# The first two batches of an attention and channel-mixing kernel: from a scheduler's order to one written out by hand on four engines

## The chip, the core and the metric

The kernel runs on one core of a Trainium2 chip. The metric is device time in microseconds; before the change the median of three runs is 1208.21 us (1207.24 to 1208.43). The core's engines run side by side, each through its own list of instructions: TensorE (PE; its weight loads are PEld), VectorE (DVE), ScalarE (ACT), GpSimd (POOL) and SyncE (SP), which issues DMAs.

## The reference

```python
# q, k, v: 8 batches x 8 heads x 576 x 64; w_phi: 64 x 128
def phi(x):
    proj = x @ w_phi
    proj = proj - max(abs(proj), axis=-1)
    return concat([exp(proj), exp(-proj)])
q_p, k_p = phi(q), phi(k)
kv, z = k_p^T v, sum_s(k_p)                  # per head
attn = (q_p kv) / (q_p z + 1e-6)
x = attn as (batch, 576, 512)
u = x + ((x^T @ U) @ V)^T                    # U 576 x 32, V 32 x 576: tokens mix
out = u + max(u @ w_ch1, 0) @ w_ch2          # 512 -> 2048 -> 512: channels mix
```

The weights U, V, w_ch1 and w_ch2 come as float64 words, and the kernel turns them into 32-bit numbers itself.

## The kernel before

**Attention.** A "pair" is two heads of one batch: four pairs (j = 0 to 3) in each of eight batches. For a pair TensorE transposes the rows of k and q (tiles T; the last 64 rows of the sequence are a tile of their own, tail_T), multiplies by w_phi (pk, pkt for k; pq, pqt for q), and VectorE and ScalarE make the features: for k the maximum of the absolute values (L367), a subtraction (L369) and two exponentials; for q a copy out of the accumulator (L387, ScalarE), an all-reduce over partitions (L388, GpSimd), a subtraction (L389, VectorE) and two exponentials (L390, L391). Then come `s_kv` (kv_ps, copied by L487) and `s_out` (xp, divided into x by L510 to L522). From the third batch on (`split`) operands are made of a high and a low part, and T and tail_T of two halves each (L302, L303).

**Tokens.** When a batch's x is whole, `Tokens` splits it into xs (`split`, L584), multiplies by U (`down`: pp, pst) and by V (`up`: vp, added to x by L614). Each half of the channels has its own `split` and `down`.

**Mixer.** Its x is transposed into uT_hi and uT_lo (L234, L235). `hidden(f)` is 12 matmuls of 128x512 into the one accumulator bank `ph` (L642), then h_hi on ScalarE (L648) and h_lo on VectorE (L649); `add(f)` is 12 matmuls into four banks `o` (L661). There are 16 f in a batch, and one `hidden` or `add` is called a chunk below. The chunks of one batch are spread between the attention steps of the next one.

**Weight blocks.** The w_ch1 and w_ch2 of each f are two blocks, 32 in all, each loaded by one DMA of 512 KB. A block passes ScalarE (L141, L145), VectorE (L142, L147, L150: the words' parts into w_b and w_r), GpSimd (L155: the sum of w_b and w_r, a 64-bit integer add), ScalarE (L227: the high part w_hi) and VectorE (L228: the low part w_lo). They are converted once, while the first two batches run. U and V go the same way, but their sum is on VectorE (L157).

**Order.** The program is written as steps, and for the first two batches a scheduler sets the order of each engine's instructions, but for `narrow` (`s_out` and the next pair's `s_kv`), whose matmuls keep their place on PE. `mix` asks for the weight blocks of f+2 as it comes to chunk f, and `Pace` spreads 28 chunks over 20 steps of the next batch. From the third batch on (`ordered`), PE keeps program order and the other engines are ordered by the scheduler. `keep_busy` issues matmuls on zeros (L741).

## Time and profile before

| | us |
|---|---|
| median of three runs | 1208.21 |
| profiled execution | 1204.81 |
| its span | 1202.7 |
| PE busy | 1141.4 |
| DVE busy | 663.1 |
| ACT busy | 528.8 |
| POOL busy | 199.5 |

The profile shows one execution, and the span is the time between its first and last instruction; 2.1 us of that execution lie outside it. PE is busy for 95% of the span, so the share alone says little: what matters is in which stretch PE is not busy. The first chunk of a Mixer starts at 122.26 us and the first matmul of the third batch's attention at 217.19 us, and the prediction divides the span at these two points. Times are read from the rows of a group of instructions ("x32 | 44.3, 1386" is 32 instructions, 44.3 us together, 1386 ns each), from a timeline (start and length of each instruction in us), and from windows (busy time of each engine in a stretch of the span).

### The profile page before, as it was taken

What the parts mean: (1) busy time and instruction counts of PE and PEld (TensorE: products, weight loads), DVE (VectorE), ACT (ScalarE), POOL (GpSimd) and SP (SyncE); (2) the same over time, 40 slices, a digit from 0 to 9 for tenths busy, and PEclk for the clock granted to TensorE, in tenths of its full rate; (3) what the DMA queues carried; (4) which work ended last, traced back from release to release, by engine and by line L of the source; (5) the groups of instructions that cost most, each with busy time, mean ns of one, the idle gap of its engine ahead of it and who ended that gap; (6) DMA issues with size and microseconds to landing.
All of it is one profiled execution on the core that took longest, in us unless ns stands there. A gap on an engine that the chain in (4) does not pass through costs nothing.

```text
span 1202.7 us, 22531 instructions
## 1 busy us (share of the span) xinstructions
PE 1141.4 (95%) x9316; PEld 949.2 (79%) x9316; DVE 663.1 (55%) x1339; ACT 528.8 (44%) x1134; POOL 199.5 (17%) x151
## 2 busy tenths in 40 slices
...
PEclk9768999999999999999999999999999999999999
...
GB/s 132 214 97 72 56 167 115 59 151 31 31 31 90 71 31 39 58 94 40 31 49 112 31 32 58 103 31 32 57 87 57 28 1 114 49 1 21 15 1 35
DMA packets 90533, 75.74 MB, mean 63 GB/s; under 512 B 51648, under 2 KB 76736, under 8 KB 90304
## 3 DMA queue, kind: packets, MB, share of 16 engines
...
q14 instruction: 27, 0.22, 0.1%
...
## 4 chain that ended last, share of the span: by engine, by line
PE 84%; DVE 9%; ACT 2%; SPq 2%; DMA 2%; issue 1%; POOL 0%; DVEq 0%; POOLq 0%
PE ph L642 31%; PE o L661 31%; PE xp L505 5%; PE kv_ps L480 4%; PE pk L437 2%; PE T L341 2%; DVE w_r L150 2%; DVE w_lo L228 1%; DMA w<-in_moe_w_ch_dram 1%; PE pp L597 1%; DVE w_r L147 1%; DVE w_b L142 1%; PE kv_ps L470 1%; PE pt L629 1%; PE pq L461 1%
## 5 line engine op out<-in xcount | busy, mean ns | idle before, releaser
L661 PE MATMUL o<-w_hi,h_hi 128*128 128x512 f32 x576 | 231.4, 402 | 4.9 <-ACT h_hi L648 4.9
L649 DVE SCALAR_TENSOR_TENSOR h_lo<-ph,h_hi 128x512 fp32r<-128x512 f32 x144 | 99.2, 689 | 246.5 <-ACT h_hi L648 246.4
L642 PE MATMUL ph<-uT_hi,w_hi 128*128 128x512 f32 x576 | 229.2, 398 | 3.8 <-DVE h_lo L649 3.1
L642 PE MATMUL ph<-uT_lo,w_hi 128*128 128x512 f32 x576 | 224.8, 390 | 0.9 <-DVE uT_lo L235 0.9
L661 PE MATMUL o<-w_lo,h_hi 128*128 128x512 f32 x576 | 225.3, 391 | 0.0
L642 PE MATMUL ph<-uT_hi,w_lo 128*128 128x512 f32 x576 | 225.2, 391 | 0.0
L661 PE MATMUL o<-w_hi,h_lo 128*128 128x512 f32 x576 | 220.4, 392 | 0.0
L648 ACT ACTIVATE h_hi<-ph 128x512 fp32r<-128x512 f32 x144 | 86.0, 597 | 273.7 <-PE ph L642 273.3
L388 POOL PARTITION_ALL_REDUCE qp<-qp x64 | 128.3, 2016 | 61.2 <-ACT qp L387 59.6
L661 PEld LDWEIGHTS o<-w_hi,h_hi 128*128 128x128 f32 x576 | 108.3, 188 | 29.0 <-ACT h_hi L648 6.3
L642 PEld LDWEIGHTS ph<-uT_hi,w_hi 128*128 128x128 f32 x576 | 108.2, 188 | 27.2 <-DVE h_lo L649 4.8
L642 PEld LDWEIGHTS ph<-uT_hi,w_lo 128*128 128x128 f32 x576 | 108.2, 188 | 24.2 <-issue 0.8
L661 PEld LDWEIGHTS o<-w_hi,h_lo 128*128 128x128 f32 x576 | 107.6, 188 | 24.2 <-issue 0.8
L642 PEld LDWEIGHTS ph<-uT_lo,w_hi 128*128 128x128 f32 x576 | 108.4, 188 | 22.0 <-DVE uT_lo L235 1.2
L388 POOL PARTITION_ALL_REDUCE qp_t<-qp_t x32 | 24.2, 757 | 606.2 <-ACT qp_t L387 606.2
L661 PEld LDWEIGHTS o<-w_lo,h_hi 128*128 128x128 f32 x576 | 108.4, 188 | 20.3 <-issue 0.8
L505 PE MATMUL xp<-kv,qp 128*64 128x65 f32 x2048 | 73.2, 232 | 12.1 <-ACT qp L390 8.5
L303 DVE TENSOR_TENSOR T<-T,T 64x512 fp32r<-64x512 f32 x96 | 66.2, 689 | 29.9 <-ACT T L302 27.2
L505 PEld LDWEIGHTS xp<-kv,qp 128*64 128x64 f32 x2048 | 68.5, 146 | 15.2 <-ACT qp L390 9.3
L302 ACT CAST T<-T 64x512 fp32r<-64x512 f32 x96 | 55.9, 582 | 36.3 <-PE T L341 19.9
L480 PE MATMUL kv_ps<-vb,kp 128*64 128x65 f32 x2048 | 67.7, 225 | 0.0
L480 PEld LDWEIGHTS kv_ps<-vb,kp 128*64 128x64 f32 x2048 | 66.7, 141 | 0.8 <-ACT qp_t L387 0.4
(128 smaller groups left out, 1499.6 us busy)
## 6 DMA issues: line engine op xcount, KB each, us to landing
w<-in_moe_w_ch_dram SPq DMA_DIRECT2D x32, 512.0 KB, 3.9
...
st<-u_dram SPq DMA_DIRECT2D x16, 512.0 KB, 4.0
...
```

The lines of the kernel that those rows point to most:

```text
L150: nc.vector.scalar_tensor_tensor(out=a, in0=hi_w, scalar=-0x80000000, in1=a, op0=ALU.bitwise_and, op1=ALU.bitwise_or)
L302: nc.scalar.copy(out=dst[0:D], in_=src)
L303: nc.vector.tensor_sub(dst[D:2 * D], src, f32(dst[0:D]))
L341: nc.tensor.transpose(out=pT[:, c * P:(c + 1) * P], in_=self.raw[n][:, c // 2, c % 2, :], identity=ident)
L388: nc.gpsimd.partition_all_reduce(qp[0], qp[1], P, ReduceOp.absmax)
L437: nc.tensor.matmul(pk[:, i, :, :], self.T[0][:, i, cs], w_hl, start=True, stop=True)
L480: nc.tensor.matmul(self.kv_v[z * HP:(z + 1) * HP, f, g, :], kp[f][:, i, z * HP:(z + 1) * HP], self.vb[:, g, t, :], start=False, stop=(t == ...
L505: nc.tensor.matmul(xv[zs, c, :], qp[f][:, c * P + z * HP:c * P + (z + 1) * HP], self.kv[:, f, c // 2, :], start=(f == 0), stop=(f == 1), s ...
L642: nc.tensor.matmul(ph, l[:, c * P:(c + 1) * P], r[:, c, :], start=(n == 0), stop=(n == len(terms) * NCC - 1))
L648: nc.scalar.activation(out=h_hi, in_=ph, func=AF.Relu)
L649: nc.vector.scalar_tensor_tensor(out=h_lo, in0=ph, scalar=0.0, in1=f32(h_hi), op0=ALU.max, op1=ALU.subtract)
L661: nc.tensor.matmul(self.o[t], l[:, cs], r, start=(f == 0 and n == 0), stop=(f == NFC - 1 and n == len(terms) - 1))
```

## The change

Pairs 0 to 6, and what is issued beside them, leave the scheduler. A new function `early` writes out their steps one after the other, and in it PE, ACT, DVE and POOL all issue in program order (`manual_schedule` on four engines); SP's DMA issues are not in that list. `ordered` then starts at pair 7 with PE alone in program order.

- A block is now loaded four blocks ahead. `begin_block` does what `convert` does, and `end_block` finishes the block before it: `join`, the sum, now on VectorE (L154) in place of GpSimd; then w_hi (L243) and w_lo (L244). `conv` calls the two.
- `transpose_both` issues all transposes of a pair and `copy_both` their copies; `whole_q` all q products, copies and all-reduces, and `end_q` the subtractions and exponentials, a step later; `whole_k` first all maxima and subtractions, then the exponentials.
- `chunk(n, blocks)` issues n chunks, with `blocks` weight blocks after each. A `hidden`'s h_hi and h_lo (now L706, L707) are held back until the next chunk's matmuls are issued, or, if that chunk is a `hidden`, until just before them.
- U and V are converted in parts; the first half of the second batch's xs gets buffers of its own; some accumulators change banks; the last two `add` of the first Mixer are split in halves as those of the others are.

```diff
--- before.py
+++ after.py
...
-    def convert(st, a, b_, wide_add=False):
+    def convert(st, a, b_):
         n = st.shape[1]
         hi_w = st[:, :, 1]
...
-        nc.scalar.activation(out=bh[:, :, 0], in_=halves[:, :, 1], func=AF.Copy, scale=2.0 ** -13)
         nc.vector.tensor_scalar(
             out=bh[:, :, 1], in0=halves[:, :, 3], scalar1=0x7FF0, scalar2=None,
             op0=ALU.bitwise_and)
+        nc.scalar.activation(out=bh[:, :, 0], in_=halves[:, :, 1], func=AF.Copy, scale=2.0 ** -13)
...
-        if wide_add:
-            a64, b64 = a.bitcast(U64), b_.bitcast(U64)
-            nc.gpsimd.int64_add(a64, a64, b64)
-        else:
-            nc.vector.tensor_tensor(out=a, in0=a, in1=b_, op=ALU.add)
+    def join(a, b_):
+        nc.vector.tensor_tensor(out=a, in0=a, in1=b_, op=ALU.add)
...
-    def weight_blocks():
...
+    NB = 2 * NFC
+    AHEAD = 4
+    loaded, begun, ended = [], [], [0]
+    def load_block():
+        i = len(loaded)
+        f, m = i // 2, i % 2 + 1
+        fs = slice(f * P, (f + 1) * P)
...
+        loaded.append(st)
+    def begin_block():
+        i = len(begun)
+        f, m = i // 2, i % 2 + 1
+        b_ = const.tile([P, C], I32, tag=f"wh{m}_{f}", name=f"w_b{m}_{f}")
+        r = const.tile([P, C], F32, tag=f"wl{i + 1}", name=f"w_r{m}_{f}")
+        convert(loaded[i], r.bitcast(I32), b_)
+        begun.append((f, m, b_, r))
+    def end_block():
+        i = ended[0]
+        f, m, b_, r = begun[i]
+        join(r.bitcast(I32), b_)
+        hi = const.tile([P, C], F32R, tag=f"wh{m}_{f}", name=f"w_hi{m}_{f}")
+        lo = const.tile([P, C], F32R, tag=f"wl{i}", name=f"w_lo{m}_{f}")
+        nc.scalar.copy(out=hi, in_=r)
+        nc.vector.tensor_sub(lo, r, f32(hi))
+        w_hi_t[m, f], w_lo_t[m, f] = hi, lo
+        begun[i] = None
+        ended[0] += 1
+    def conv(n=1):
+        for _ in range(n):
+            while len(loaded) < min(len(begun) + AHEAD, NB):
+                load_block()
+            if len(begun) < NB:
+                begin_block()
+            if ended[0] < len(begun) - 1 or len(begun) == NB and ended[0] < NB:
+                end_block()
...
+        def transpose_both(self):
+            nm = self.nm
...
+            nc.gpsimd.memset(self.tail_T, 0.0)
+            self.pT = []
+            for n in self.order():
+                pT = self.ps(f"T{n}_", True)
+                for c in range(NT):
+                    nc.tensor.transpose(
+                        out=pT[:, c * P:(c + 1) * P], in_=self.raw[n][:, c // 2, c % 2, :],
+                        identity=ident)
+                self.pT.append(pT)
+            self.tT = self.ps("tT")
+            nc.tensor.transpose(out=self.tT[:, 0:2 * ST], in_=self.t_r, identity=ident)
...
+        def copy_both(self):
+            nc.scalar.copy(out=self.T[self.order()[0]], in_=self.pT[0])
+            for g in range(2):
+                r_ = slice(g * D, (g + 1) * D)
+                nc.scalar.copy(
+                    out=self.tail_T[r_, :, r_],
+                    in_=self.tT[r_, 0:2 * ST].rearrange("p (n r) -> p n r", n=2))
+            nc.scalar.copy(out=self.T[self.order()[1]], in_=self.pT[1])
+            self.pT = self.tT = None
...
+        def q_finish(self, qps):
+            for qp in qps:
+                nc.vector.tensor_sub(qp[1], qp[1], qp[0])
+                self.both_exp(qp)
...
+        def whole_k(self):
+            pt = self.ps("pkt")
+            nc.tensor.matmul(pt[:, 0:F], self.tail_T[:, 0, :], w_f, start=True, stop=True)
             pks = [self.ps(f"pk{r}_", True) for r in range(2)]
...
+            self.kpt = self.k_features(
+                "t", pt[:, 0:F].unsqueeze(1), self.k_tile("t", 1), False)
             self.kp = [
                 self.k_features(
-                    r, pks[r].rearrange("p (t f) -> p t f", f=F), self.k_tile(r, NT))
+                    r, pks[r].rearrange("p (t f) -> p t f", f=F), self.k_tile(r, NT), False)
                 for r in range(2)]
-        def project_q_whole(self):
+            for kp in (self.kpt, *self.kp):
+                self.both_exp(kp)
...
+        def whole_q(self):
             pqs = [self.ps(f"pq{r}_", True) for r in range(2)]
...
+            pt = self.ps("pqt")
+            nc.tensor.matmul(pt[:, 0:2 * ST], w_f, self.tail_T[:, 1, :], start=True, stop=True)
+            self.qp = [self.q_features(r, pqs[r], SM, False) for r in range(2)]
+            self.qpt = self.q_features("t", pt, 2 * ST, False)
+        def end_q(self):
+            self.q_finish((self.qpt, *self.qp))
...
-                if b == 0:
-                    xs = home(("xs", t), (2, C // 2), f"xs{b}_{i}_{t}", F32R)
+                if b == 0 or b == 1 and i == 0:
...
-        def hidden(self, f):
+        def hidden(self, f, later=False):
...
+            if later:
+                return lambda: self.relu(f, ph)
+            self.relu(f, ph)
+        def relu(self, f, ph):
...
+    ORDERED = 7
+    held = []
+    def chunk(n=1, blocks=0):
+        for _ in range(n):
+            fn, f, *ts = todo.pop(0)
+            rest = held.pop() if held else None
+            if rest is not None and fn.__name__ == "hidden":
+                rest()
+                rest = None
+            if fn.__name__ == "hidden":
+                held.append(fn(f, True))
+            else:
+                fn(f, *ts)
+                if rest is not None:
+                    rest()
+            conv(blocks)
+    def early(x, xt):
+        p = [Pair(*pairs[0])]
+        load_w_phi(w_f)
+        p[0].load_v()
+        p.append(Pair(*pairs[1]))
+        p[1].load_v()
+        p.append(Pair(*pairs[2]))
+        uv = uv_parts()
+        next(uv)
+        keep_busy(6)
+        p[0].transpose_both()
+        p[0].copy_both()
+        p[0].whole_q()
+        p[0].whole_k()
+        tk = Tokens(0, x, xt)
+        for i in range(NPAIR - 1):
+            if i < 2:
+                p.append(Pair(*pairs[i + 3]))
+            p[i + 1].transpose_both()
+            keep_busy(2)
+            p[i].end_q()
+            p[i + 1].copy_both()
+            if i == 1:
+                next(uv)
+            p[i].s_kv()
+            p[i + 2].load_v()
+            keep_busy(2)
+            if i == 2:
+                next(uv)
+            p[i + 1].whole_q()
+            p[i + 1].whole_k()
+            if i == 2:
+                tk.down(0)
+            p[i].s_out(x, xt)
+            keep_busy(2)
+            if i == 1:
+                next(uv)
+                tk.split(0)
+            if i == 2:
+                next(uv, None)
+                conv()
+        p[4].transpose_both()
+        p.append(Pair(*pairs[NPAIR + 1]))
+        keep_busy(2)
+        p[3].end_q()
+        p[4].copy_both()
+        p[3].s_kv()
+        p[5].load_v()
+        p[3].s_out(x, xt)
+        keep_busy(2)
         tk.split(1)
...
+        p[4].whole_k()
+        conv()
         tk.down(1)
...
+        p[4].whole_q()
+        conv()
+        for t in range(NT):
+            tk.up(t)
+        m = Mixer(0, x)
         m.transposes(0)
+        m.transposes(1)
+        conv()
         tk.up(NT)
-        mix()
-        m.transposes(1)
         m.transposes(2)
-        mix()
         m.transposes(3)
+        p[4].end_q()
+        conv(2)
         todo.extend(m.chunks())
-        while fill:
-            other()
-    ORDERED = 2
+        chunk(1, 1)
+        p[4].s_kv()
+        chunk(1, 1)
+        x = moe.tile([P, NT, C], F32, tag="x", name="x1")
+        tk = Tokens(1, x, xt)
+        for i in range(5, 8):
+            p[i].transpose_both()
+            p[i].copy_both()
+            p.append(Pair(*pairs[i + 1]))
+            p[i + 1].load_v()
+            chunk(1, 1)
+            p[i].whole_k()
+            chunk(2, 1)
+            with tc.manual_schedule(engines={nc.tensor.engine}):
+                p[i - 1].s_out(x, xt)
+                p[i].s_kv()
+            if i == 6:
+                tk.split(0)
+            chunk(1, 1)
+            p[i].whole_q()
+            chunk(1, 2)
+            if i == 6:
+                tk.down(0)
+            p[i].end_q()
+            chunk(1, 1)
+            if i == 7:
+                p[8].transpose_k()
+            chunk(1, 1)
+        while ended[0] < NB:
+            conv()
+        while held:
+            held.pop()()
+        return p[7], p[8], x, xt, tk
...
-    def ordered(cur, nxt, x, xt, tk):
-        for n, (b, j) in list(enumerate(pairs))[ORDERED * NPAIR:]:
+    def ordered(cur, nxt, x, xt, tk, far):
+        for n, (b, j) in list(enumerate(pairs))[ORDERED:]:
             last = j == NPAIR - 1
-            far = Pair(*pairs[n + 2]) if n + 2 < len(pairs) else None
+            if far is None and n + 2 < len(pairs):
+                far = Pair(*pairs[n + 2])
+                far.load_v()
...
-    if True:
-        cur = Pair(0, 0)
-        load_w_phi(w_f)
-        cur.load_v()
-        keep_busy(6)
...
-        for n, (b, j) in enumerate(pairs[:ORDERED * NPAIR]):
-            far = Pair(*pairs[n + 2]) if n + 2 < len(pairs) else None
-            if far is not None:
-                far.load_v()
-            step(nxt.s_k0)
-            if nxt.split:
-                step(nxt.s_k1)
-                nxt.transpose_q()
-            step(narrow, nxt, cur, x, xt)
...
-        with tc.manual_schedule(engines={nc.tensor.engine}):
-            mix(2)
-            ordered(cur, nxt, x, xt, tk)
+    x = moe.tile([P, NT, C], F32, tag="x", name="x0")
+    xt = moe.tile([P, C], F32, tag="xt", name="xt0")
+    nc.vector.memset(xt[ST:P], 0.0)
+    with tc.manual_schedule(
+            engines={e.engine for e in (nc.tensor, nc.scalar, nc.vector, nc.gpsimd)}):
+        cur, nxt, x, xt, tk = early(x, xt)
+    with tc.manual_schedule(engines={nc.tensor.engine}):
+        ordered(cur, nxt, x, xt, tk, None)
```

On VectorE the weight blocks stood mixed, as the scheduler found them free. At the end of the first batch before:

```order
L142 TENSOR_SCALAR w_b_1_1380<-w_1_1378 128x512
L150 SCALAR_TENSOR_TENSOR w_r_0_1367<-w_0_1364,w_r_0_1367 128x512
L147 TENSOR_SCALAR w_r_1_1381<-w_1_1378 128x512
L142 TENSOR_SCALAR w_b_1_1394<-w_1_1392 128x512
L147 TENSOR_SCALAR w_r_1_1395<-w_1_1392 128x512
L150 SCALAR_TENSOR_TENSOR w_r_1_1381<-w_1_1378,w_r_1_1381 128x512
L150 SCALAR_TENSOR_TENSOR w_r_1_1395<-w_1_1392,w_r_1_1395 128x512
L142 TENSOR_SCALAR w_b_2_1408<-w_2_1406 128x512
L228 TENSOR_TENSOR w_lo_0_1361<-w_r_0_1353,w_hi_0_1360 128x512
L147 TENSOR_SCALAR w_r_2_1409<-w_2_1406 128x512
```

With the change, in the middle of the second batch, a block is three instructions, the sum (ISA) and the low part of the block before it, and then the next one; h_lo of a chunk stands between two blocks:

```order
L707 SCALAR_TENSOR_TENSOR h_lo_3_1605<-ph_3_1550,h_hi_3_1604 128x512
L141 TENSOR_SCALAR w_b_6_1610<-w_6_1416 128x512
L147 TENSOR_SCALAR w_r_6_1611<-w_6_1416 128x512
L150 SCALAR_TENSOR_TENSOR w_r_6_1611<-w_6_1416,w_r_6_1611 128x512
L154 ISA w_r_5_1566<-w_r_5_1566,w_b_5_1565 128x1024
L244 TENSOR_TENSOR w_lo_5_1619<-w_r_5_1566,w_hi_5_1618 128x512
L141 TENSOR_SCALAR w_b_6_1624<-w_6_1446 128x512
L147 TENSOR_SCALAR w_r_6_1625<-w_6_1446 128x512
L150 SCALAR_TENSOR_TENSOR w_r_6_1625<-w_6_1446,w_r_6_1625 128x512
L154 ISA w_r_6_1611<-w_r_6_1611,w_b_6_1610 128x1024
L244 TENSOR_TENSOR w_lo_6_1633<-w_r_6_1611,w_hi_6_1632 128x512
L444 TENSOR_TENSOR qp_1_t<-qp_1_t 128x128
```

What moved: the sum is new on this engine, w_lo stands right behind it, and the q subtractions (L444) and h_lo (L707) have fixed places behind whole blocks.

On GpSimd the 64-bit sums stood between the all-reduces (L388) of the second batch:

```order
L388 ISA qp_0_t<-qp_0_t 128x128
L388 ISA qp_0_0_1112<-qp_0_0_1112 128x512
L388 ISA qp_0_1_1118<-qp_0_1_1118 128x512
L155 ISA w_r_6_1817<-w_r_6_1817,w_b_6_1816 128x512
L155 ISA w_r_6_1803<-w_r_6_1803,w_b_6_1802 128x512
L155 ISA w_r_5_1670<-w_r_5_1670,w_b_5_1669 128x512
L316 MEMSET tail_T_2_1583 128x256
L388 ISA qp_1_t<-qp_1_t 128x128
L388 ISA qp_1_0_1508<-qp_1_0_1508 128x512
L388 ISA qp_1_1_1514<-qp_1_1_1514 128x512
```

With the change only the all-reduces (now L437) and the clearing of tail_T (L356) are left:

```order
L437 ISA qp_0_0_1087<-qp_0_0_1087 128x512
L437 ISA qp_0_1_1090<-qp_0_1_1090 128x512
L437 ISA qp_0_t<-qp_0_t 128x128
L356 MEMSET tail_T_1_1309 128x256
L437 ISA qp_1_0_1583<-qp_1_0_1583 128x512
L437 ISA qp_1_1_1586<-qp_1_1_1586 128x512
L437 ISA qp_1_t<-qp_1_t 128x128
L356 MEMSET tail_T_2_1702 128x256
```

What moved: 32 sums left this engine, and the order of an all-reduce's pieces changed (the tail last).

On PE, ahead of the first matmul of the third batch's attention (pkt from w_hl), f = 9 was the last `hidden` and f = 8 the last `add`:

```order
L642 MATMUL ph_9_2355<-uT_hi_1184,w_hi_9_2092 128x512
L642 MATMUL ph_9_2355<-uT_lo_1185,w_hi_9_2092 128x512
L642 MATMUL ph_9_2355<-uT_hi_1184,w_lo_9_2093 128x512
L661 MATMUL o_0_1520<-w_hi_8_2008,h_lo_8_2295 128x512
L661 MATMUL o_1_1521<-w_hi_8_2008,h_lo_8_2295 128x512
L661 MATMUL o_2_1522<-w_hi_8_2008,h_lo_8_2295 128x512
L661 MATMUL o_3_1523<-w_hi_8_2008,h_lo_8_2295 128x512
L399 MATMUL pkt_0_2383<-w_hl,tail_T_0_2300 128x128
L400 MATMUL pkt_0_2383<-w_hl,tail_T_0_2300 128x128
```

With the change the last ones there are f = 11 and f = 10:

```order
L719 MATMUL o_1_1340<-w_hi_10_2086,h_lo_10_2409 128x512
L719 MATMUL o_2_1341<-w_hi_10_2086,h_hi_10_2408 128x512
L719 MATMUL o_2_1341<-w_lo_10_2087,h_hi_10_2408 128x512
L719 MATMUL o_2_1341<-w_hi_10_2086,h_lo_10_2409 128x512
L719 MATMUL o_3_1342<-w_hi_10_2086,h_hi_10_2408 128x512
L719 MATMUL o_3_1342<-w_lo_10_2087,h_hi_10_2408 128x512
L719 MATMUL o_3_1342<-w_hi_10_2086,h_lo_10_2409 128x512
L451 MATMUL pkt_0_2536<-w_hl,tail_T_0_2474 128x128
L452 MATMUL pkt_0_2536<-w_hl,tail_T_0_2474 128x128
L499 MATMUL pk_2_0_2552<-w_hl,T_2_0_2480 128x256 x2
L499 MATMUL pk_2_0_2557<-w_hl,T_2_0_2480 128x256 x2
```

What moved: two `hidden` and two `add` more stand ahead of that matmul.

More of the change, by code (lines that the diff above doesn't have):

```diff
@@ L179, in load_uv @@
             nc.sync.dma_start(out=sv[g * ST:(g + 1) * ST, NT], in_=U[SM:S])
+        cs3 = (slice(0, SM // 2), slice(SM // 2, SM), slice(SM, S))
+        v_st = []
+        for cs in cs3:
+            sv, sgo = staged(f"v_st{cs.start}", cs.stop - cs.start)
+            for g in range(4):
+                nc.sync.dma_start(out=sv[g * R:(g + 1) * R], in_=V[:, cs])
+            v_st.append(sgo)
+        yield
         u_f = go().rearrange("p (t r) -> p t r", r=R)
@@ L189, in load_uv @@
                 nc.vector.tensor_copy(out=u_all[pr, to, i, :], in_=f32(u_all[pr, to, 0, :]))
[L191 to L195 removed]
+        for cs, go in zip(cs3, v_st):
+            yield
             v_f = go()
@@ L288, in ps @@
         def ps(self, name, late=False):
-            return ps(f"{name}{self.nm}", "o" if late and self.b == 0 else "at")
+            return ps(f"{name}{self.nm}", "o" if late and self.free else "at")
         def load_v(self):
@@ L343, in transpose @@
                     identity=ident)
-            if self.split:
-                m = att.tile([P, 2, SM], F32R, tag="T", name=f"T{n}_{self.nm}")
-                for s in range(2):
-                    self.stack(pT[s * D:(s + 1) * D, :], m[:, s, :])
-            else:
-                nc.scalar.copy(out=m, in_=pT)
+            m = att.tile([P, 2, SM], F32R, tag="T", name=f"T{n}_{self.nm}")
+            for s in range(2):
+                self.stack(pT[s * D:(s + 1) * D, :], m[:, s, :])
             return m
@@ L696, in chunks @@
             return todo
-    blocks = weight_blocks()
-    done_f = [-1]
-    def weights(upto):
-        while done_f[0] < upto:
-            done_f[0] = next(blocks, NFC)
     todo = []
```

208 lines of the change are left out of this document (52 added, 156 removed).

## The prediction

> **What bounds the kernel now.** The page's first lines and its slices come first:
>
> ```profile
> span 1202.7 us, 22531 instructions
> PE 1141.4 (95%) x9316; PEld 949.2 (79%) x9316; DVE 663.1 (55%) x1339; ACT 528.8 (44%) x1134; POOL 199.5 (17%) x151
> PEclk9768999999999999999999999999999999999999
> ```
>
> PE lacks 61 us of the span. The windows (length; busy time by engine; granted clock; DMA share; GB/s) tell where:
>
> ```profile
> 0.00:122.26 122.26, 82.55 (x926) 61.06 (x926) 92.50 (x196) 79.79 (x167) 46.35 (x50) 0.82 0.43 128
> 122.26:217.19 94.93, 86.49 (x748) 67.20 (x748) 72.12 (x133) 59.58 (x113) 35.19 (x25) 0.98 0.34 104
> 217.19:300.00 82.81, 77.00 (x611) 63.35 (x610) 52.49 (x103) 38.46 (x81) 14.86 (x10) 1.00 0.27 87
> 300.00:1000.00 700.00, 699.70 (x6154) 595.51 (x6153) 405.60 (x850) 326.21 (x731) 103.06 (x66) 1.00 0.17 51
> 39.00:75.00 36.00, 17.01 (x154) 12.66 (x153) 35.60 (x58) 28.01 (x51) 18.24 (x12) 0.59 0.58 189
> 185.00:217.00 32.00, 25.80 (x197) 19.16 (x194) 31.72 (x54) 21.55 (x39) 15.24 (x10) 0.95 0.29 87
> ```
>
> PE is idle for 39.7 us before 122.26, 8.4 from there to 217.19, 5.8 to 300, and 0.3 in the next 700. So the kernel is matmul bound from about 217 on, and only the part before it can give much. There VectorE is the full engine: 35.6 of 36 us in 39 to 75, 31.7 of 32 in 185 to 217. The timeline of PE fixes my two marks, the first `hidden` and the first matmul of the third batch's attention (mark M), and the length of a chunk (139.53 to 142.26 holds 12 matmuls: 2.73 us):
>
> ```profile
> 122.26 0.50 PE L642 MATMUL ph<-uT_hi,w_hi 128*128 128x512 f32 x1
> 217.19 0.22 PE L399 MATMUL pkt<-w_hl,tail_T 128*128 128x128 f32 x1
> 139.53 0.39 PE L642 MATMUL ph<-uT_hi,w_hi 128*128 128x512 f32 x1
> ```
>
> Two groups of PE's up to M count chunks (shortest, median, longest; first and last start):
>
> ```profile
> L642 PE MATMUL ph<-uT_hi,w_hi x40: 387/391/501, 122.3 to 215.6; 128*128 128x512 f32 x40
> L661 PE MATMUL o<-w_hi,h_hi x36: 387/394/588, 128.8 to 211.8; 128*128 128x512 f32 x36
> ```
>
> Four of each stand in a chunk, so 10 `hidden` and 9 `add` are done at M.
>
> **The sum's frame.** The change has 12 and 11 ahead of M: 4 chunks of 2.73 us, 10.9 us of PE's work, need not be done after it. What follows M is the same program; its 5.8 us of idle time up to 300 fall where blocks were still being converted, and these are now done, so I take 4.3 of them away (bounds 0 and 5.5). With T the new time of M: span = 1202.7 - 217.19 - 10.9 - 4.3 + T = T + 970.3. The execution's own time is 2.1 above its span and 3.4 below the median shown, so the time to forecast is T + 975.8. No change is T = 232.4. T has two stages: to the last uT_lo of the first Mixer, and from there to M.
>
> **Stage 1, now 123.6 us (the last of the uT_lo).** What it rests on, by group (count; busy us, mean ns; idle before):
>
> ```profile
> L388 POOL PARTITION_ALL_REDUCE qp<-qp x24 | 48.9, 2069 | 36.9 <-ACT qp L387 36.7
> L388 POOL PARTITION_ALL_REDUCE qp_t<-qp_t x12 | 9.4, 784 | 96.4 <-ACT qp_t L387 96.4
> L387 ACT COPY qp<-pq 128x512 f32<-128x512 f32 x24 | 13.4, 584 | 6.5 <-PE pq L424 5.7 <-PE pq L462 0.8
> L389 DVE TENSOR_TENSOR qp<-qp 128x512 f32<-128x512 f32 x16 | 14.0, 875 | 2.7 <-POOL qp L388 2.4
> L390 ACT ACTIVATE qp<-qp 128x512 f32<-128x512 f32 x24 | 15.1, 629 | 17.0 <-DVE qp L389 17.0
> L367 DVE TENSOR_REDUCE mk<-pk 128x4 f32<-128x512 f32 x16 | 10.6, 683 | 3.9 <-PE pk L411 3.9
> L516 DVE TENSOR_TENSOR x<-xp,den 128x256 f32<-128x256 f32 x22 | 9.3, 421 | 0.4
> L584 DVE TENSOR_TENSOR xs<-xt,xs 128x256 fp32r<-128x256 f32 x5 | 2.1, 414 | 0.0
> ```
>
> and one row of ScalarE's timeline, the end of pair 0's copies:
>
> ```profile
> 7.21 0.59 ACT L349 COPY T<-T 128x512 f32<-128x512 f32 x1 [0.27 <-PE T L341]
> ```
>
> In program order a pair is a ring, because `copy_both` of the next pair stands behind `end_q`'s exponentials on ScalarE: copies of T and tail_T 1.7, the first q copy 0.6, three all-reduces 2 x 2.05 + 0.75 = 4.8, the subtraction that gates 0.9, exponentials 4 x 0.63 + 2 x 0.3 = 3.1. That is 11.1 us, and the next pair's transposes are issued ahead of it. Pair 0's T stands at 7.8; with q copies, all-reduces, subtraction and exponentials its features end at about 18. Pair 1 is then at 29.6. Pairs 2 and 3 are longer, since VectorE also converts U (2.7) and V (2.4, sums of many small instructions), makes k features (four of 0.68 and small ones, 3.2), outputs (two of 0.42 and small ones, 2.1) and xs (five of 0.42, 2.1), and waits about 3 for ScalarE's part of U: 17.6 and 15.8, to 63.0. What stays is serial on VectorE and PE: the second `split`, `down`, three blocks, `up` and the four transposes' uT_lo, 24 us; and 2 for VectorE operations that an all-reduce holds up (stage 2). Stage 1 ends at **89**, an estimate by walk through the order. Bounds: VectorE's own work, 62 us behind a start of 10, gives 72; the ring with its matmuls and waits at the pace of 39 to 75 (clock 0.59) gives about 105.
>
> **Stage 2, now 94 us.** Here 27 blocks, 23 chunks, three and a bit pairs. The rows of a block:
>
> ```profile
> L155 POOL INT64_ADD w_r<-w_r,w_b x32 | 44.3, 1386 | 90.0 <-DVE w_r L150 59.7 <-ACT w_b L145 18.0 <-ACT qp L390 2.7
> L228 DVE TENSOR_TENSOR w_lo<-w_r,w_hi 128x512 fp32r<-128x512 f32 x32 | 27.6, 862 | 5.7 <-ACT w_hi L227 5.3
> L150 DVE SCALAR_TENSOR_TENSOR w_r<-w,w_r 128x512 int32<-128x512 int32 x32 | 25.7, 811 | 0.1
> L142 DVE TENSOR_SCALAR w_b<-w 128x512 uint16<-128x512 uint16 x32 | 23.5, 733 | 3.8 <-DMA w<-in_moe_w_ch_dram 2.5 <-PE pq L424 1.2
> L147 DVE TENSOR_SCALAR w_r<-w 128x512 int32<-128x512 int32 x32 | 19.8, 624 | 2.8 <-PE pp L597 2.8
> L227 ACT CAST w_hi<-w_r 128x512 fp32r<-128x512 f32 x32 | 19.5, 611 | 7.5 <-POOL w_r L155 7.5
> L649 DVE SCALAR_TENSOR_TENSOR h_lo<-ph,h_hi 128x512 fp32r<-128x512 f32 x28 | 19.3, 688 | 30.0 <-ACT h_hi L648 29.9
> L157 DVE CUSTOM_DVE_ANT_0 v_st<-v_st 128x512 uint16<-128x512 uint16 x2 | 0.8, 406 | 0.0
> L157 DVE CUSTOM_DVE_ANT_0 u_st<-u_st 128x320 uint16<-128x320 uint16 x1 | 0.3, 326 | 0.6 <-ACT u_st L145 0.6
> ```
>
> and of the timelines of VectorE and GpSimd (start, length):
>
> ```profile
> 186.34 0.46 DVE L142 TENSOR_SCALAR w_b<-w 128x512 uint16<-128x512 uint16 x1
> 186.69 0.41 DVE L147 TENSOR_SCALAR w_r<-w 128x512 int32<-128x512 int32 x1
> 187.02 0.68 DVE L150 SCALAR_TENSOR_TENSOR w_r<-w,w_r 128x512 int32<-128x512 int32 x1
> 188.23 1.27 DVE L142 TENSOR_SCALAR w_b<-w 128x512 uint16<-128x512 uint16 x1
> 187.88 1.29 POOL L155 INT64_ADD w_r<-w_r,w_b  x1 [3.28 <-DVE w_r L150]
> 168.79 0.41 DVE L147 TENSOR_SCALAR w_r<-w 128x512 int32<-128x512 int32 x1
> 169.23 0.69 DVE L150 SCALAR_TENSOR_TENSOR w_r<-w,w_r 128x512 int32<-128x512 int32 x1
> ```
>
> Removed: the sum on GpSimd. The same L142 takes 0.46 alone and 1.27 while the sum at 187.88 runs, ending with it. Over 32 blocks L150 (0.81 against 0.68), L142 (0.73 against 0.46), L147 (0.62 against 0.41) and L228 (0.86 against 0.68) lose 0.79 us a block, 25 in all. All-reduces do the same, so that 3 us remain in my sum. The Trainium skill ("SBUF — State Buffer", section "Who interferes with whom") has VectorE and GpSimd share a port pair that one holds for its whole instruction; the rows agree, L142 waits out the sum. By a rule so strict three pairs' all-reduces could cost VectorE 8 us, 5 more than my sum holds, and the time would be 1207.6.
>
> Added: the sum on VectorE. No sum of this size is in the trace. From 160 to 256 numbers it grows by 80 ns, 0.83 ns a number: 0.62 us for 512 (bounds 0.41, the smaller one, and 0.81, its double). I take 0.62. On VectorE one block is then, from start to start, 0.35 + 0.44 (L150 needs L147) + 0.60 + 0.62, then w_lo, which stands right behind the sum and so waits for ScalarE to make w_hi of it: 0.61 + 0.07, and 0.60 itself. That is 3.26 us, and 0.75 of it VectorE stands still. Behind it there stand the next block, h_lo and the q subtractions. 27 x 3.26 = 88.
>
> The rest of VectorE: h_lo 11 x 0.6 = 6.6; k features 3 x 3.2, outputs 3 x 2.1, kv copies 1.6, q subtractions 4 x 1.5, xs, pst, the two parts of w_phi and the stacks of T and tail_T 4.7, together 28.2. Waits, where w_hi stands on ScalarE behind something else: behind T's copies, whose transposes stand on PE behind a chunk, 2.0 at each of three pairs; behind exponentials, 0.6 at each of three pairs' k and 1.05 at each of four q, 6.0. With 3 for the all-reduces: 88 + 6.6 + 28.2 + 12 + 3 = **138**. Bounds: 106 without the stand-still (27 x 0.75) and the waits, 155 with a sum of 0.81 and waits twice as long.
>
> T = 89 + 138 = 227, and the time 227 + 975.8 = **1202.6** (from 226.8). Stage 1 gains 35 and stage 2 gives 44 back, of which 15.2 (10.9 + 4.3) is work and idle time that is then gone behind M.
>
> Transposes, loads of U and V and the `keep_busy` are costed at nothing: PE has 97 us of work in stage 2 (86.5 busy now, and four chunks) for 138. The weight loads hide behind VectorE, four blocks ahead; without that cover each costs a transfer (the last rival but one).
>
> **The rivals.**
>
> *VectorE's bound holds in stage 1 (0.20).* The ring is overlapped, stage 1 ends at 72: T = 210, 1186. For it: 35.6 of 36 us busy in 39 to 75. Against: a strict order, and all-reduces that nothing on VectorE waits out.
>
> *The sum is dear (0.13).* At 0.81 and no less waiting: 27 x 0.19 = 5 us, 1207.7, no change.
>
> *PE's clock falls in stage 2 (0.20); slower.* `ph` is one bank: `hidden(f+1)` can't start until h_lo(f) has read it, and h_lo stands behind a block. PE then works in bursts with gaps, and the clock was 0.59 where it was busy for 17.0 of 36 us. PE's 97.4 us last 138 at a clock of 0.71; below it PE decides. At 0.65 they last 150 (1214.6), at 0.59 165 (1229.9). Against: at 25.8 of 32 us busy the clock was 0.95.
>
> The Trainium skill ("TensorE: Matmul & The Clock Gate", Part 1) has half speed only after an idle window of about 3.4 us. Gaps here would be under 3 us; by it this rival falls away and the sum stays 1202.6.
>
> *Loads come late (0.07); slower.* SP's list isn't hand ordered: a block's load behind one that waits for PE delays VectorE, and everything behind it in program order. One load late at each of three pairs, at the 3.9 us that a block's load takes from issue to landing, is 11.7 us, 1214.3:
>
> ```profile
> w<-in_moe_w_ch_dram SPq DMA_DIRECT2D x32, 512.0 KB, 3.9
> ```
>
> *The change doesn't order what it says.* The order of instructions shows that it does; 0.
>
> **How the numbers follow.** My forecast has 0.40, with 1195 to 1209 as its own range (stage 1 from 82 to 95). A measurement of this kernel tells 0.2% (2.4 us: 1205.8 to 1210.6) from no change. Faster: 0.33 of the 0.40 and 0.20, 0.53. Same: 0.06 and 0.10, 0.16. Slower: 0.01, 0.03, 0.20 and 0.07, 0.31. The range, 1183 to 1220, takes in the faster rival and the milder half of the slower ones.
>
> **What would show it.** The first `hidden` near 88 us (right: stage 1), M near 227 with VectorE over 90% busy ahead of it; the sum at 0.62 us; w_lo with 0.7 us idle ahead of it that w_hi ends; L141, L147, L150 at 0.46, 0.41, 0.68; PE's clock above 0.9 from 89 on; idle after M under 2 us. Wrong: M before 212 or behind 236, or a gap on VectorE that a DMA ends.

## The result: 1.2% slower

The changed kernel takes 1222.66 us (1221.27 to 1223.45), the kernel before, beside it, 1207.72: a ratio of 1.0123 (95% interval 1.0106 to 1.0141). One execution of a later run, with w_phi moved ahead, took 6322 us and is left out of its figure. The forecast was 1202.6 with a range to 1220, and the other sign.

The page of the kernel after, and its windows up to and behind the first `hidden` (93.9) and the mark M (244.65):

```profile
span 1220.3 us, 22461 instructions
PE 1134.9 (93%) x9292; PEld 948.3 (78%) x9300; DVE 669.6 (55%) x1371; ACT 537.4 (44%) x1134; POOL 153.3 (13%) x119
```

```profile
0.00:93.88 93.88, 62.97 (x802) 48.50 (x811) 62.71 (x153) 59.06 (x126) 26.81 (x36) 0.81 0.42 121
93.90:244.60 150.70, 108.29 (x894) 84.81 (x894) 111.63 (x219) 95.81 (x166) 15.47 (x11) 0.85 0.35 109
```

Stage 1 is indeed 28 us shorter (122.3 before). Stage 2 is 56 us longer (94.9 before), and in it no engine is full: PE is idle for 42 us, VectorE for 39, ScalarE for 55. The waits of VectorE and of PE in stage 2 (what waited, for what: us in all, times, longest):

```profile
DVE w_lo L244 <- ACT w_hi L243: 24.0, 27, 1.8
DVE h_lo L707 <- ACT h_hi L706: 11.7, 6, 4.1
```

```profile
PE ph L695 <- DVE h_lo L707: 28.6, 6, 9.1
PE pkt L451 <- DVE tail_T L331: 10.9, 1, 10.9
```

In the kernel before, VectorE's two waits for the same instructions are short (122.26 to 217.19 us):

```profile
DVE h_lo L649 <- ACT h_hi L648: 7.4, 4, 3.1
DVE w_lo L228 <- ACT w_hi L227: 4.1, 2, 2.2
```

One block on VectorE's timeline shows the unit of it: three starts, the sum, 0.74 us of standing still for ScalarE's w_hi, the low part, 3.44 us in all up to the next instruction:

```profile
117.21 0.46 DVE L141 TENSOR_SCALAR w_b<-w 128x512 uint16<-128x512 uint16 x1
117.55 0.41 DVE L147 TENSOR_SCALAR w_r<-w 128x512 int32<-128x512 int32 x1
118.00 0.69 DVE L150 SCALAR_TENSOR_TENSOR w_r<-w,w_r 128x512 int32<-128x512 int32 x1
118.61 0.69 DVE L154 CUSTOM_DVE_ANT_0 w_r<-w_r,w_b 128x1024 uint16<-128x1024 uint16 x1
120.04 0.69 DVE L244 TENSOR_TENSOR w_lo<-w_r,w_hi 128x512 fp32r<-128x512 f32 x1 [0.74 <-ACT w_hi L243]
120.65 0.28 DVE L412 TENSOR_REDUCE mk_t<-pkt 128x1 f32<-128x128 f32 x1
```

Where did stage 1's 28 us come from? Not from a better packing. VectorE's idle time there is 29.8 us before (122.26 - 92.50) and 31.2 after. What left is work: up to the first `hidden` the group of a block's first VectorE instruction counts 14 before and 4 after:

```profile
L142 DVE TENSOR_SCALAR w_b<-w 128x512 uint16<-128x512 uint16 x14 | 9.7, 696 | 1.5 <-PE pq L424 1.2 <-DMA w<-in_moe_w_ch_dram 0.2
```

```profile
L141 DVE TENSOR_SCALAR w_b<-w 128x512 uint16<-128x512 uint16 x4 | 2.5, 620 | 0.1
```

Ten blocks moved from stage 1 to stage 2, where each costs 3.4 us with its standing still.

### The profile page after: what moved, and what is told of

It is laid out like the page before. It is cut to its first block, busy times and chain, and to the rows that moved or that the text cites. A ratio compares the mean times of both kernels' runs of the same rounds, so it can differ in the third digit from the quotient of the medians.

```text
span 1220.3 us, 22461 instructions
## 1 busy us (share of the span) xinstructions
PE 1134.9 (93%) x9292; PEld 948.3 (78%) x9300; DVE 669.6 (55%) x1371; ACT 537.4 (44%) x1134; POOL 153.3 (13%) x119
## 4 chain that ended last, share of the span: by engine, by line
PE 80%; DVE 11%; ACT 5%; SPq 2%; issue 1%; DMA 1%; ACTq 0%; DVEq 0%
PE ph L695 30%; PE o L719 29%; PE xp L564 5%; PE kv_ps L539 4%; PE pk L499 2%; PE T L389 2%; PE pp L650 1%; PE pt L682 1%; ACT w_hi L243 1%; DVE w_r L154 1%; DVE w_lo L244 1%; DVE w_r L150 1%; PE pq L520 1%; PE xp L557 1%; PE kv_ps L529 1%
## 5 line engine op out<-in xcount | busy, mean ns | idle before, releaser
L695 PE MATMUL ph<-uT_hi,w_hi 128*128 128x512 f32 x576 | 235.8, 409 | 36.8 <-DVE h_lo L707 33.9
L707 DVE SCALAR_TENSOR_TENSOR h_lo<-ph,h_hi 128x512 fp32r<-128x512 f32 x144 | 99.3, 690 | 282.6 <-ACT h_hi L706 282.6
L706 ACT ACTIVATE h_hi<-ph 128x512 fp32r<-128x512 f32 x144 | 85.8, 596 | 333.2 <-PE ph L695 332.5
L695 PE MATMUL ph<-uT_lo,w_hi 128*128 128x512 f32 x576 | 229.8, 399 | 0.7 <-DVE uT_lo L262 0.7
L695 PE MATMUL ph<-uT_hi,w_lo 128*128 128x512 f32 x576 | 229.1, 398 | 0.0
L719 PE MATMUL o<-w_hi,h_lo 128*128 128x512 f32 x576 | 225.0, 391 | 0.0
L695 PEld LDWEIGHTS ph<-uT_hi,w_hi 128*128 128x128 f32 x576 | 111.1, 193 | 63.4 <-DVE h_lo L707 37.2
L437 POOL PARTITION_ALL_REDUCE qp<-qp x64 | 128.1, 2013 | 213.0 <-ACT qp L436 212.4
L695 PEld LDWEIGHTS ph<-uT_hi,w_lo 128*128 128x128 f32 x576 | 110.9, 192 | 24.6
L695 PEld LDWEIGHTS ph<-uT_lo,w_hi 128*128 128x128 f32 x576 | 111.3, 193 | 22.1 <-DVE uT_lo L262 1.3
L437 POOL PARTITION_ALL_REDUCE qp_t<-qp_t x32 | 24.3, 759 | 636.0 <-ACT qp_t L436 636.0
L564 PE MATMUL xp<-kv,qp 128*64 128x65 f32 x2048 | 68.5, 227 | 0.0
L564 PEld LDWEIGHTS xp<-kv,qp 128*64 128x64 f32 x2048 | 65.8, 144 | 0.0
```

The lines of the kernel that those rows point to most:

```text
L437: nc.gpsimd.partition_all_reduce(qp[0], qp[1], P, ReduceOp.absmax)
L564: nc.tensor.matmul(xv[zs, c, :], qp[f][:, c * P + z * HP:c * P + (z + 1) * HP], self.kv[:, f, c // 2, :], start=(f == 0), stop=(f == 1), s ...
L695: nc.tensor.matmul(ph, l[:, c * P:(c + 1) * P], r[:, c, :], start=(n == 0), stop=(n == len(terms) * NCC - 1))
L706: nc.scalar.activation(out=h_hi, in_=ph, func=AF.Relu)
L707: nc.vector.scalar_tensor_tensor(out=h_lo, in0=ph, scalar=0.0, in1=f32(h_hi), op0=ALU.max, op1=ALU.subtract)
L719: nc.tensor.matmul(self.o[t], l[:, cs], r, start=(f == 0 and n == 0), stop=(f == NFC - 1 and n == len(terms) - 1))
```

## The experiments

The ratios are to the kernel before, measured beside each run. Two questions come first: which of the change's two parts, the sum's engine or the order, costs; and what in stage 2 holds the engines up.

### The sum alone, and what it gains

The kernel before, with one line changed:

```diff
-                convert(st, r.bitcast(I32), b_, True)
+                convert(st, r.bitcast(I32), b_)
```

> The kernel before with one part of the change alone: the sum on VectorE, the order left to the scheduler. Theory S: VectorE loses 25 us of hold-ups and gains 32 x 0.61 = 20 us of sums: within 5 us of 1207.7 us. If the sum on VectorE by itself were what made the change slower: 1213-1223 us.

Measured: 1192.63 us, ratio 0.9878 (0.9862 to 0.9895). Both expectations fell: it is 14.4 us faster. So the sum on VectorE is a clear gain by itself, and the rest of the change (the hand-written order, and the conversion of U and V, buffers and banks that go with it) loses 30 us against it. M comes at 208.1 (first and last start in the row of pkt), and VectorE's instructions lose their hold-ups:

```profile
L399 PE MATMUL pkt<-w_hl,tail_T x24: 220/220/327, 208.1 to 951.1; 128*128 128x128 f32 x24
```

```profile
L157 DVE CUSTOM_DVE_ANT_0 w_r<-w_r,w_b 128x1024 uint16<-128x1024 uint16 x32 | 22.8, 714 | 0.7 <-ACT w_b L145 0.3
L228 DVE TENSOR_TENSOR w_lo<-w_r,w_hi 128x512 fp32r<-128x512 f32 x32 | 22.1, 691 | 2.1 <-ACT w_hi L227 2.0
L150 DVE SCALAR_TENSOR_TENSOR w_r<-w,w_r 128x512 int32<-128x512 int32 x32 | 21.8, 684 | 0.2
```

Is that the hold-ups, or the block's way over GpSimd that is gone? The same kernel, with an add of the old size on GpSimd beside each block, on a load buffer that is done with, so that the block waits for nothing; the result does not use it:

```diff
                 convert(st, r.bitcast(I32), b_)
+                s64 = st.rearrange("p c w -> p (c w)")[:, 0:C].bitcast(U64)
+                nc.gpsimd.int64_add(s64, s64, s64)
```

> The kernel before with the sum on VectorE, and beside it a 64-bit add of the old sum's size on GpSimd for each block, on a load buffer that is done with, so that nothing of the block waits for it (the result does not use it; its buffer is free 1.4 us later). Theory H (what the sum on VectorE gains is the hold-ups that GpSimd's add causes on VectorE, 0.8 us a block): the gain goes and more, 1205-1215 us. Theory W (the gain is the block's way over GpSimd, 1.4 us and the queue behind the all-reduces): 1191-1197 us, as without the add.

Measured: 1212.33 us, ratio 1.0040 (1.0023 to 1.0057), 19.7 us slower than without the add, and slower than the kernel before. VectorE's instructions are long again, the sum among them (GpSimd's group first):

```profile
L226 POOL INT64_ADD w<-w x32 | 39.7, 1242 | 86.0 <-DVE w_r L150 41.4 <-DVE den L513 9.9 <-ACT qp_t L389 6.0
L157 DVE CUSTOM_DVE_ANT_0 w_r<-w_r,w_b 128x1024 uint16<-128x1024 uint16 x32 | 30.5, 955 | 0.8 <-ACT w_b L145 0.5
L230 DVE TENSOR_TENSOR w_lo<-w_r,w_hi 128x512 fp32r<-128x512 f32 x32 | 25.7, 804 | 1.4 <-ACT w_hi L229 1.4
L150 DVE SCALAR_TENSOR_TENSOR w_r<-w,w_r 128x512 int32<-128x512 int32 x32 | 25.5, 800 | 0.1
```

By a dependency the add makes later only the freeing of a load buffer, and on GpSimd itself the all-reduces behind it. Neither shows as a longer wait: up to M VectorE waits 4.0 us for all-reduces, where it waited 8.8 us without the adds, and 3.4 us for blocks' loads, where it waited 4.3. What grows is VectorE's busy time up to M (without the adds, then with them), by 22.7 us, while its idle time stays near 50 and M comes 19.7 us later:

```profile
0.00:208.20 208.20, 172.06 (x1675) 130.71 (x1682) 155.83 (x351) 137.84 (x277) 47.38 (x47) 0.89 0.41 123
0.00:227.80 227.80, 175.58 (x1690) 130.69 (x1697) 178.50 (x358) 142.18 (x283) 77.95 (x75) 0.88 0.37 112
```

The means of the five groups of a block (L142 and L147 with 66 and 92 ns, the three shown with 241, 113 and 116) rose by 0.63 us together, 20 us over 32 blocks. So the add costs through VectorE. That the two sums agree so closely is in part luck: stage by stage they do not agree, since the first `hidden` comes only 2.4 us later (119.6 against 117.2) although 14 of the blocks are begun ahead of it. The scheduler's order shifts with such an edit, and how much of the 19.7 us is its doing is not shown. The Trainium skill ("SBUF — State Buffer", section "Who interferes with whom") has VectorE and GpSimd share a port pair, which the one that issues first holds for its whole instruction while the other blocks. The trace agrees: L150 takes 0.80 us beside the adds, 0.68 without.

The reverse, the hand order with the sum back on GpSimd, issued right behind a block's first part:

```diff
         convert(loaded[i], r.bitcast(I32), b_)
+        a64, b64 = r.bitcast(I32).bitcast(U64), b_.bitcast(U64)
+        nc.gpsimd.int64_add(a64, a64, b64)
...
-        join(r.bitcast(I32), b_)
```

> The changed kernel with the sum back on GpSimd as a 64-bit add, issued right behind a block's first part; order otherwise as in the change. Theory S: a block on VectorE loses the sum (0.61) and the stand-still (0.74, since the high part is ready a block later) and gains some 0.8 of hold-ups while GpSimd adds: 27 x 0.55 = 15 us less before M, 1206-1210 us. Theory K: less than 6 us, above 1216 us. If moving the sum off GpSimd were what the change gains by, this would be slower than 1223 us.

Measured: 1225.59 us, ratio 1.0157 (1.0141 to 1.0172), 2.9 us slower than the change; my theory had 13 to 17 us faster. The low part now runs beside the add and takes 1.43 us instead of 0.69, which is more than the sum that VectorE saves, and it still waits 23.1 us for w_hi (stage 2, VectorE's groups):

```profile
L245 DVE TENSOR_TENSOR w_lo<-w_r,w_hi 128x512 fp32r<-128x512 f32 x28 | 40.1, 1434 | 23.1 <-ACT w_hi L244 23.1
```

That wait I had missed: w_hi stands on ScalarE behind the next block's L144 and L145 (0.78 and 0.87 us), and L145 itself waits for VectorE's L141 (27.8 us in all), so w_hi is late whenever the sum is done.

### Which engines' program order costs

The change's steps and PE's list as they are, but the other three engines given to the scheduler:

```diff
-            engines={e.engine for e in (nc.tensor, nc.scalar, nc.vector, nc.gpsimd)}):
+            engines={nc.tensor.engine}):
```

> The changed kernel with its steps and PE's program order as they are, but ACT, DVE and POOL ordered by the scheduler. Theory L: the loss lies in the program order of those three; M at 205-218, 1181-1194 us. If the order of the steps, or PE's program order, were the cause: above 1215 us.

Measured: 1209.37 us, ratio 1.0019 (1.0006 to 1.0033); between the two expectations. M is at 230.1, 14.5 us earlier than in the change. The first `hidden` is at 117.5, where the kernel before with the sum on VectorE has it (117.2): the scheduler takes blocks back into stage 1, 19 begun in place of 4. The remaining 16.7 us to the kernel before with the sum on VectorE lie in the order of steps, PE's list or the change's other parts as the scheduler meets them; which of these isn't settled. It is no fixed price of theirs, since the same steps and PE's list come to 1200.00 us further down.

ScalarE alone given to the scheduler (`engines` without `nc.scalar`):

> The changed kernel with ScalarE alone given back to the scheduler; PE, DVE and POOL keep program order. If ScalarE's program order (h_hi behind copies of T, copies of q and high parts that wait for VectorE's sum) carries most of the lockstep: 1203-1212 us. If VectorE's does: 1217-1223 us.

Measured: 1223.67 us, ratio 1.0143 (1.0119 to 1.0168), no gain. The wait only changed its place, from h_hi to w_hi:

```profile
DVE w_lo L244 <- ACT w_hi L243: 31.5, 28, 4.1
DVE h_lo L707 <- ACT h_hi L706: 2.8, 1, 2.8
```

### VectorE's standing still

The low part issued one block later, so that it no longer stands behind its own sum:

```diff
         nc.scalar.copy(out=hi, in_=r)
-        nc.vector.tensor_sub(lo, r, f32(hi))
-        w_hi_t[m, f], w_lo_t[m, f] = hi, lo
+        w_hi_t[m, f] = hi
+        lows.append((m, f, i, r, hi))
...
+            while lows:
+                low_part()
             if ended[0] < len(begun) - 1 or len(begun) == NB and ended[0] < NB:
                 end_block()
```

> The changed kernel, with the low part of a block (L244) issued one block later, so that it no longer stands right behind its own sum. Theory S (VectorE in program order sets the second stage, and a quarter of it is VectorE standing still): the 24.0 us of waiting for w_hi before the mark M go, M moves from 244.65 to 222-228 us, the time from 1222.7 to 1200-1206 us. Theory K (the one accumulator bank of `hidden` and TensorE's low clock set it): VectorE waits for h_hi instead, M moves by less than 6 us, the time stays above 1216 us.

Measured: 1211.63 us, ratio 1.0037 (1.0024 to 1.0051); M at 233.9. Between the two: 11 us of the 24. No wait for w_hi is left, but the one for h_hi has doubled:

```profile
DVE h_lo L719 <- ACT h_hi L718: 23.6, 10, 5.6
DVE T L343 <- ACT T L342: 2.3, 2, 1.6
```

On ScalarE, h_hi stands behind w_hi, and w_hi waits for VectorE's sum: the round trip is still there, one instruction further on.

Is it TensorE's side, its one `ph` bank, that PE waits 28.6 us for? h_hi and h_lo not held back, in the change and with the low part later:

```diff
-                held.append(fn(f, True))
+                fn(f)
```

> The changed kernel without holding h_hi and h_lo back: they are issued right behind their own `hidden`, ahead of the weight block that follows it. Theory L (lockstep: with one `ph` bank, `hidden`, h_hi, h_lo and the blocks stand in each engine's program order so that the engines wait for each other in turn): PE's 28.6 us of waiting for h_lo fall below 10, M moves from 244.65 to 230-237, the time is 1207-1215 us. Theory V (only VectorE's own work and its 24 us of standing still count): VectorE waits for h_hi instead, 1219-1224 us.

> Both edits at once: the low part one block later, and h_hi and h_lo not held back. Theory L: VectorE's 110 us of work in the second stage are then nearly its length, M at 215-224, 1191-1200 us. Theory V: as with the low part alone, 1208-1214 us.

Measured: 1221.86 us (ratio 1.0125, 1.0104 to 1.0146) and 1211.82 us (1.0047, 1.0028 to 1.0066): nothing. PE's waits for h_lo fell to 6.8 and 6.7 us, as theory L wanted, and others took their place: in the first PE then stood 13.9 us at M, and 8.8 at pkt. PE's waits are where VectorE's lateness shows, not what makes it: whichever of them is taken away, PE stands at M for VectorE's tail_T (10.9 us in the change, 13.9 and 12.9 here).

Now w_hi moved on as well: sum, a block later w_hi, a block later the low part; then again with h_hi and h_lo not held back:

```diff
             if len(begun) < NB:
                 begin_block()
+            if highs:
+                low_part()
+            if joined:
+                high_part()
             if ended[0] < len(begun) - 1 or len(begun) == NB and ended[0] < NB:
                 end_block()
```

> The changed kernel with both ScalarE's high part (w_hi) and VectorE's low part moved on by one block each: a block is summed, its high part is made one block later and its low part after that, so that neither engine's list has an instruction right behind the one of the other engine that it needs. Theory R (round trips: in program order an instruction that waits for the other engine holds up all that stands behind it, h_hi behind w_hi above all; moving only the low part moved the wait from w_lo to h_lo): VectorE's 24 us for w_hi and most of the 12 to 24 us for h_hi go, M at 213-222, 1188-1199 us. Theory P (PE, its one `ph` bank and its low clock hold the stage at about 140 us whatever the blocks do): M at 230-236, 1207-1213 us, as with the low part alone.

> The same with h_hi and h_lo not held back. Theory R: as the run before within 3 us, or up to 5 us faster, since h_lo then stands ahead of a block. Theory P: 1207-1213 us.

Measured: 1202.00 us (ratio 0.9961, 0.9948 to 0.9973) and 1200.00 us (0.9944, 0.9922 to 0.9966): 20.7 and 22.7 us faster than the change, and both now faster than the kernel before. M is at 225.5 and 222.3, where theory R had 213 to 222, and the times are 3 and 1 us above its range: R, with less than all of its gain, and not P. In the second, the waits of VectorE and PE in stage 2 (`issue` is a wait for nothing that the profile shows):

```profile
DVE h_lo L727 <- ACT h_hi L726: 17.4, 11, 2.4
DVE T L351 <- ACT T L350: 0.6, 1, 0.6
```

```profile
PE pkt L478 <- issue: 6.5, 2, 6.1
PE ph L715 <- DVE h_lo L727: 5.6, 2, 4.7
```

Of 36.9 us that VectorE stood still, 18.3 are left, nearly all of it for h_hi. Setting the round trips of the weight blocks apart gives back 20.7 of the 30 us that the change loses against the kernel before with the same sum, and 22.7 with h_hi and h_lo not held back; this is shown. (About 1 us of it is only put off: 28 low parts are done at M in place of 30.)

### Fewer blocks before M

```diff
-            chunk(1, 2)
+            chunk(1, 1)
```

> The changed kernel with one block in place of two after one chunk of each of the three pairs, so that three blocks fewer are converted before M and three more after it. Theory S: M moves by 3 x 3.3 = 10 us, and VectorE has room behind M: 1212-1215 us. Theory K: no change, 1220-1224 us.

> The same again with one block in place of two after one chunk of each of the three pairs. Theory R: VectorE then sets the stage, and three blocks of 2.7 us are 8 us less before M: 1180-1192 us. Theory P: no change against the run before.

Measured: 1219.21 us (ratio 1.0102, 1.0086 to 1.0117), a third of the 10 us; and 1200.89 us (0.9951, 0.9932 to 0.9969), nothing. In both PE then stood at M for the two parts of w_phi, here in the second:

```profile
PE pkt L471 <- DVE w_hl L100: 15.4, 1, 15.4
```

L100 comes behind the last blocks, because the load of w_phi takes one of the four load buffers that the blocks hold. Moved ahead, behind pair 7's q products:

```diff
             p[i].whole_q()
+            if i == 7:
+                split_w()
             chunk(1, 1)
```

> The hand order with all edits so far (high and low part later, h_hi and h_lo not held back, three blocks fewer before M), and the two parts of w_phi for the third batch loaded and split right behind pair 7's q products, and no longer behind the last blocks: in the run before this one TensorE stood 15.4 us at M for them, VectorE's L100 having waited for a load buffer that the blocks held. If that wait ate what the three blocks gave: M at 208-214, 1187-1193 us. If VectorE's amount of work sets M: 1197-1201 us.

Measured: 1200.05 us, ratio 0.9943 (0.9926 to 0.9959): no change. M is at 217.6, 4.7 us earlier than with all blocks (222.3), but the rest of the span is 981.5 in place of 975.5. Blocks put off behind M are paid for there.

### The loss behind M

In the changed kernel PE waits for h_lo at every later batch's border; before, and with the sum alone, it does not. Windows from 300 to 1190 us, the changed kernel, then the kernel before:

```profile
PE ph L695 <- DVE h_lo L707: 4.0, 5, 0.8
```

```profile
PE ph L642 <- DVE h_lo L649: 0.3, 1, 0.3
```

PE's list explains it. Before, the second half of the last `add` of a Mixer stands between the next Mixer's first two `hidden`; in the hand order one chunk more is done at each border, that half stands ahead of both, and nothing covers h_lo. The last chunk of the hand-written part left to `ordered`, its block kept:

```diff
             if i == 7:
                 p[8].transpose_k()
-            chunk(1, 1)
+                conv()
+            else:
+                chunk(1, 1)
```

> The hand order with high and low part later and h_hi and h_lo not held back, and with the last chunk of the hand-written part left to `ordered` (its weight block stays). From the third batch on PE's list then has the last half of a Mixer's last `add` between the next Mixer's first two `hidden` again, as the kernel before has; in the hand order that half stands ahead of both, and the second `hidden` waited for h_lo, 0.8 us in five batches and 1.2 in one, 5.3 us in all. If that place is the cause: those waits go, 1194-1197 us. If they come from the state that the first batches leave behind: they stay, 1199-1202 us.

Measured, on top of w_hi and the low part later and nothing held back (1200.00): 1196.43 us, ratio 0.9901 (0.9885 to 0.9918), 3.6 us faster than without it. The waits are gone; behind M one is left:

```profile
PE ph L715 <- DVE h_lo L727: 0.4, 1, 0.4
```

This is the best of the hand orders. The kernel before with the sum on VectorE, one line, has the lowest time of all (1192.63, ratio 0.9878), but the two intervals overlap, so the hand order is not shown to be slower than it.

## Why the prediction was wrong, step by step

The time came out 20 us above the forecast, and each part of the sum was short: stage 1 by 6.4 us, stage 2 by 11.3, the frame by 2.2. The kind of loss, VectorE standing still for ScalarE behind a fixed order, was in the sum; what failed is the size of the terms, one by one.

**The frame** (T + 975.8) was 2.2 us short. Behind M the span is 975.65 where it had 970.3, and the span lies 2.4 us below the median shown where it had 5.5. The idle time right behind M did go as taken (5.8 us in the first 83 before, 1.4 after). But five waits, 4.0 us in all, came in at the later borders: the extra chunks that I counted as a credit also moved the phase of the chunks, which I did not look at. That step is shown by the last run. And PE, which had stood for 10.9 us at M, ran at a low clock right behind it, so that its busy time behind M fell by 8.8 us and not by 10.9:

```profile
244.65:255.00 10.35, 10.35 (x66) 8.69 (x68) 9.40 (x19) 6.66 (x15) 0.00 (x0) 0.77 0.23 74
```

**Stage 1** had 89; the first `hidden` is at 93.9, the last uT_lo ends at 95.4. The ring was right in kind. The last exponential of each of the first four pairs shows where it fell short:

```profile
15.98 0.63 ACT L423 ACTIVATE qp<-qp 128x512 f32<-128x512 f32 x1
27.44 0.63 ACT L423 ACTIVATE qp<-qp 128x512 f32<-128x512 f32 x1
48.31 0.63 ACT L423 ACTIVATE qp<-qp 128x512 f32<-128x512 f32 x1
67.13 0.63 ACT L423 ACTIVATE qp<-qp 128x512 f32<-128x512 f32 x1
```

Pair 1 ends at 28.1 (forecast 29.6), but pairs 2 and 3 then take 20.9 and 18.8 us where the prediction had 17.6 and 15.8: this is the step of stage 1 that failed. What follows pair 3 took 27.6 us for 26. V's sum also waits for ScalarE, not only U's (the prediction had 3 for U and nothing for V); that is half of the 6.3 us by which pairs 2 and 3 are longer, and the rest is not divided further:

```profile
DVE u_st L154 <- ACT u_st L145: 3.4, 1, 3.4
DVE v_st L154 <- ACT v_st L145: 3.1, 1, 3.1
```

The reading "stage 1 gains 35" misled me beside that. It is no error of the sum, which has the 27 blocks of stage 2, but I called a gain what the order of instructions and the counts show as ten blocks carried over.

**Stage 2** had 138 and took 149.3 (95.4 to 244.65). By terms: the sum is 0.69 where I took 0.62, and as w_hi and the low part follow it, a block is 3.44 where I had 3.26 (my parts add up to 3.29): 27 x 0.18 = 5 us. The wait for h_hi was 11.7 where I had 6.0 for T's copies; this term was mis-sized the most. The wait for w_hi was 24.0, where I had 20 for the standing still and 6 for the exponentials. The all-reduces' hold-ups were near: L141, L147 and the sum, 40, 70 and 50 ns longer than alone on average, 27 x 0.16 = 4.4, against 3 (and not the 8 of the stricter rule, for which the prediction names no rows). These make 10 of the 11 us. So the mechanism was right, and most sizes were short. My sign "VectorE over 90% busy" went against my own sum, which has it standing still for 32 of 138 us; it was busy for 110 of 149, 74%.

**Removed and added: the sum.** On VectorE it came out as worked out: the means of L142, L147, L150 and the low part fell by 0.73 us a block (0.79 predicted), 23 us, against 0.61 from start to start for the sum, 20. (The prediction's L142 does not end with the sum beside it, but 0.33 us later, at 189.50 against 189.17.) But I took it that the time follows VectorE's net, 3 to 5 us, and that part alone gave 14.4. The runs show which price was wrong. With the sum on VectorE and adds left on GpSimd the kernel is only 4.9 us slower than the kernel before (1212.33 against 1207.45 beside it), where I had put 20 us of sums; without the adds it is 19.7 us faster than that. So the hold-ups count about in full, and the sum for well under half of its length; whether that is the block's way over GpSimd, which goes with it, or the scheduler's new order isn't settled. In the traces M comes 9.1 us earlier (217.2, 208.1), with one `add` more and two low parts fewer done ahead of it, and VectorE has been busy for 155.8 us up to it in place of 164.6; the profiled execution, 1196.46 us, was the slowest of its kernel's and shows 8.3 of the 14.4. I also weighed this part and the order in one sum on VectorE, and so could not see that one gains 14 and the other loses 30.

**The rivals.** *PE's clock*, at 0.20, had times around the right one (1214.6 to 1229.9) and signs that came true: a clock of 0.85 in stage 2, gaps on PE behind h_lo. That was luck. By its own working PE decides only below a clock of 0.71, and at M PE stood for VectorE. With the gaps behind h_lo cut from 28.6 to 6.8 us PE stood elsewhere and the time stayed, and with VectorE's round trips set apart the time fell by 22.7 us while the clock went from 0.85 to 0.90 (stage 2 of that run):

```profile
93.00:222.30 129.30, 103.38 (x892) 81.77 (x890) 108.93 (x215) 92.28 (x165) 17.62 (x11) 0.90 0.41 124
```

My reason against it was wrong too: gaps on PE of up to 10.9 us did occur, where I had them under 3. Behind one of 6.7 us the `hidden` starts a matmul every 0.43 us, where at full clock 12 take 2.73 us, 0.23 each. The Trainium skill ("TensorE: Matmul & The Clock Gate", Part 1) has half speed after an idle window of about 3.4 us; these rows agree.

```profile
109.11 0.79 PE L695 MATMUL ph<-uT_hi,w_hi 128*128 128x512 f32 x1 [6.70 <-DVE h_lo L707]
109.70 0.63 PE L695 MATMUL ph<-uT_lo,w_hi 128*128 128x512 f32 x1
110.13 0.63 PE L695 MATMUL ph<-uT_hi,w_lo 128*128 128x512 f32 x1
```

*The sum is dear* was half right (0.69, not 0.81). *VectorE's bound holds in stage 1* fell, and *loads come late* too: no wait of VectorE's in stage 2 ends with a DMA. What the rivals lacked was the kind that decided: not one slow engine, but three lists in fixed order, each with an instruction that waits for the next one.
